# Attention and routed experts on one core: the fifth unit's scores move into a shared PSUM bank, and minima go head by head

## The chip, the cores and the metric

The kernel runs on one core of a Trainium2 chip. The metric is the time of one execution in microseconds, on the device. TensorE (PE) multiplies matrices into PSUM, which has eight banks of 128 partitions by 512 float32 columns here; VectorE (DVE), ScalarE (ACT) and GpSimd (POOL) work on what lies there and in SBUF; SyncE (SP) issues the loads. Each engine runs its own instructions in their order and waits on semaphores for the others.

## The reference, cut to what matters

```
scores = scale * q @ k.T                        # B=8, H=8, S=576, D=64
scores = where(0 <= i - j < 128, scores + slope_h * -|i - j|, -1e9)
attn   = exp(scores - max) / (sum + 1e-9)       # per row
x      = (attn @ v), heads side by side         # 4608 x 512
choice = greedy routing of x @ w_gate, 8 experts with 576 places each
out[e's rows] = relu(x[rows] @ w1[e]) @ w2[e]
```

Only the attention is touched by the change. Since the window is 128 wide, a block of 64 queries meets three blocks of 64 keys at most.

## The kernel before

**Pairs and units.** Two heads h = 0, 1 of one batch are a pair; there are 32 pairs n, four to a batch. Of a pair, q and k lie in one tile with head h on partitions 64h to 64h+63, which is the row group of PE that its matmuls use. The nine blocks of 64 queries are grouped in five units. Units 0 to 3 hold two blocks each, r = 0 and r = 1, and each head's scores of them fill one bank, s[0] or s[1], block r on partitions 64r and up. Unit 4 holds the one block that is left, for both heads: its scores lie in s[0] on partitions 0 to 63 for head 0, and in s[1] on partitions 64 to 127 for head 1, behind the columns of units 0 and 1. It has 192 columns in the pairs of even batches and 64 in those of odd batches; unit 0 has 128 and 192.

**Scores come in two halves** (`UNITS`, L22): units 2 and 3, then units 0, 1 and 4. `scores(n, half)` (L106) takes two banks of `ps_s`, which has only these two, so each half reuses the banks of the half before once its minima have been read; pairs 0 and 1 take banks of `ps_t` for their second half. Its matmuls alternate between the heads (`HR`): (h, r) = 00, 10, 01, 11.

**Minima.** `least(n, units)` (L122) is one DVE instruction for each unit and head, which scales the scores, adds the bias, writes the result to `u` and the row's minimum to `mn` (an accumulator read follows each, as an instruction of its own). Unit 4 takes two such instructions of 64 partitions, since its two heads lie in two banks. `exps` (L138) makes the weights in place, on ACT. Both go unit by unit, head 0 and head 1 in turn.

**One iteration n of the loop** puts on PE, in this order: the transposes of units 2, 1 and 3 of pair n-2 (`turn`, L150, each into a `ps_t` bank, pt); `natural(n-4)` (L224), the output turned back, ten passes named pt L53; the transposes of unit 0 of n-2; the first half of the scores of n; the 64 x 64 transposes of unit 4 of n-2; `av(n-3)` (L167), weights times values, into two banks of `ps_x`, x[0] and x[1]; and the second half of the scores of n. On DVE stand, in the same iteration: minima of units 0 and 1 of n-1, the copy PT1 of unit 1's transposes (`turned`, L162), the minima of unit 4 of n-1, the copy PT3, the minima of units 2 and 3 of n, `divide(n-4)`, and small steps of the router. ACT copies x of n-4 out (L213) and the transposes of units 2 and 0, beside the exponentials; POOL moves 64 columns of that copy (L215).

**What sets the order.** The program keeps the written order on each engine (`put`). Which bank of `ps_t` a tile gets follows the order in which banks come free. A bank x[0] uses its columns 0 to 319 alone. Every float32 matmul shows as two passes in the trace.

The first lines of `scores` and the one of `unit` that place unit 4:

```
        s = [bank() if half and n < 2 else ps_s.tile([128, 512], F32, name="s") for _ in range(2)]
        for t in UNITS[half]:
...
        if t == 4:
            return ms, 64 * m0 + 192, 128 * m0 + 384, 1216 - 64 * ms
```

## Time and profile before

| | us |
|---|---|
| three runs | 699.79, 700.03, 702.93 |
| their median | 700.03 |
| the profiled execution | 701.81 |
| its span in the trace | 700.0 |
| PE busy | 667.7 (95%) |
| PE weight loads busy (PEld) | 589.3 (84%) |
| DVE busy | 465.1 (66%) |
| ACT busy | 326.8 (47%) |
| POOL busy | 152.0 (22%) |
| minima, L133, 308 instructions, mean 332 ns | 88.6 |
| exponentials, L144, 288 instructions, mean 436 ns | 123.9 |
| scores, L53, 1112 passes, mean 327 ns | 65.8 |

The attention fills about the first 214 us of the span; the rest is the last of the routing and the two layers of the experts. The shares of the page are taken over the whole span and don't say what limits the attention. That is read from the chain of waits and the timelines of that stretch, where a row gives the start of a group of instructions, the time from its start to its end, the engine, the line and the tiles. PE's passes overlap, so the time of one (327 ns) is far longer than the time from one to the next.

### The profile page before, as it was taken

What the parts mean: (1) busy time and instruction counts of PE and PEld (TensorE: products, weight loads), DVE (VectorE), ACT (ScalarE), POOL (GpSimd) and SP (SyncE); (2) the same over time, 40 slices, a digit from 0 to 9 for tenths busy, and PEclk for the clock granted to TensorE, in tenths of its full rate; (3) what the DMA queues carried; (4) which work ended last, traced back from release to release, by engine and by line L of the source; (5) the groups of instructions that cost most, each with busy time, mean ns of one, the idle gap of its engine ahead of it and who ended that gap; (6) DMA issues with size and microseconds to landing.
All of it is one profiled execution on the core that took longest, in us unless ns stands there. A gap on an engine that the chain in (4) does not pass through costs nothing.

```text
span 700.0 us, 18965 instructions
## 1 busy us (share of the span) xinstructions
PE 667.7 (95%) x7266; PEld 589.3 (84%) x7267; DVE 465.1 (66%) x1940; ACT 326.8 (47%) x991; POOL 152.0 (22%) x337
## 2 busy tenths in 40 slices
PE   8999999999992899999999999999999999999996
PEld 4899999998981688789788889889988988988985
DVE  5789888888977889699578829828846524523210
ACT  6798888888952344234133233214314324323210
POOL 4022221222220303223250231132133023011011
PEclk8999999999996899999999999999999999999998
DMA  8456575665421725435064234146135325301001
GB/s 297 147 177 208 177 222 175 218 197 180 160 71 45 231 73 189 165 123 209 34 210 133 79 111 160 60 135 181 35 128 162 114 91 154 104 30 38 1 24 49
DMA packets 35139, 92.72 MB, mean 132 GB/s; under 512 B 3808, under 2 KB 13152, under 8 KB 35040
## 3 DMA queue, kind: packets, MB, share of 16 engines
q1 hardware_dynamic: 29152, 72.55, 31.9%
q0 software_dynamic: 5888, 18.88, 8.3%
q8 instruction: 59, 0.97, 0.6%
q14 instruction: 40, 0.33, 0.1%
HBM read 72.54 MB, written 18.87 MB: 131 GB/s over the span
## 4 chain that ended last, share of the span: by engine, by line
PE 84%; DVE 9%; issue 3%; DMA 2%; ACT 1%; SPq 0%; POOL 0%; POOLq 0%; DVEq 0%
PE ph L951 25%; PE po L980 10%; PE po L981 10%; PE s L53 8%; PE po L983 8%; PE pt L157 6%; PE pt L53 6%; PE x L53 6%; PE pg L928 2%; DVE hl L895 2%; DMA raw<-in_w_dram 1%; DVE u L133 1%; DVE hlo L962 1%; ACT hl L893 1%; PE x L1134 1%
## 5 line engine op out<-in xcount | busy, mean ns | idle before, releaser
L951 PE MATMUL ph<-xh,hl 128*128 128x288 f32 (+2 forms) x1024 | 189.7, 298 | 0.0
L951 PEld LDWEIGHTS ph<-xh,hl 128*128 128x128 f32 x1024 | 154.3, 189 | 1.0
L980 PE MATMUL po<-hl,hh 128*128 128x512 f32 (+1 forms) x328 | 130.7, 398 | 0.0
L144 ACT ACTIVATE u<-u,mn 128x192 f32<-128x192 f32 (+2 forms) x288 | 123.9, 436 | 6.2 <-DVE mn L133 6.0
L981 PE MATMUL po<-hl,hh 128*128 128x512 f32 (+1 forms) x328 | 126.4, 385 | 0.0
L951 PE MATMUL ph<-xl,hl 128*128 128x288 f32 (+2 forms) x512 | 115.7, 298 | 0.0
L957 ACT ACTIVATE hh<-ph 128x288 fp32r<-128x288 f32 (+2 forms) x128 | 46.9, 408 | 145.7 <-PE ph L951 139.6
L133 DVE CUSTOM_DVE_ANT_0 u<-s,bm 128x192 f32<-128x192 f32 x308 | 88.6, 332 | 27.0 <-PE s L53 14.8
L983 PE MATMUL po<-hl,hlo 128*128 128x512 f32 (+1 forms) x264 | 102.0, 386 | 0.0
L895 DVE TENSOR_TENSOR hl<-raw,hl 128x512 fp32r<-128x512 f32 x128 | 84.8, 682 | 13.2 <-ACT hl L893 12.8
L992 POOL DMA_INDIRECT out_dram<-o,idx x40 | 43.8, 1094 | 203.2 <-ACT o L987 125.0
L951 PEld LDWEIGHTS ph<-xl,hl 128*128 128x128 f32 x512 | 84.1, 189 | 0.1
L932 DVE TENSOR_TENSOR xl<-pg,xh 128x512 fp32r<-128x512 f32 (+1 forms) x37 | 23.7, 640 | 83.7 <-ACT xh L931 82.6
L962 DVE SCALAR_TENSOR_TENSOR hlo<-ph,hh 128x288 fp32r<-128x288 f32 (+2 forms) x128 | 49.8, 416 | 40.7 <-ACT hh L957 39.5
L893 ACT CAST hl<-raw 128x1024 fp32r<-128x1024 f32 x64 | 65.5, 1049 | 16.6 <-DMA raw<-in_w_dram 10.8
L980 PEld LDWEIGHTS po<-hl,hh 128*128 128x128 f32 x328 | 61.7, 188 | 11.1
L981 PEld LDWEIGHTS po<-hl,hh 128*128 128x128 f32 x328 | 61.8, 188 | 10.6
L53 PE MATMUL s<-qk 64*64 64x192 f32 (+1 forms) x1112 | 65.8, 327 | 1.1 <-DVE mn L133 0.6
L987 ACT COPY o<-po 128x512 f32<-128x512 f32 (+1 forms) x33 | 18.9, 573 | 95.0 <-PE po L983 60.1
L904 POOL DMA_INDIRECT g<-x,idx x40 | 43.8, 1095 | 83.4 <-PE pg L928 33.8
L983 PEld LDWEIGHTS po<-hl,hlo 128*128 128x128 f32 x264 | 49.6, 188 | 10.1
L157 PE MATMUL pt<-ident_sb,u 128*128 128x128 f32 x368 | 53.7, 282 | 1.9 <-DVE PT L165 1.5
(233 smaller groups left out, 925.2 us busy)
## 6 DMA issues: line engine op xcount, KB each, us to landing
raw<-in_w_dram SPq DMA_DIRECT2D x64, 512.0 KB, 3.4
qk<-in_qk_dram SPq DMA_DIRECT2D x32, 576.0 KB, 5.0
v<-in_v_dram SPq DMA_DIRECT2D x32, 288.0 KB, 4.0
x<-xb SPq DMA_DIRECT2D x14, 512.0 KB, 3.6
x<-xb SPq DMA_DIRECT2D x8, 128.0 KB, 2.8
x<-xb SPq DMA_DIRECT2D x4, 256.0 KB
g<-x,idx POOLq DMA_INDIRECT x40
out_dram<-o,idx POOLq DMA_INDIRECT x40
```

What stands on the lines that cost most here:

```text
L53: put(nc.tensor.matmul(out, w, a, start=start, stop=stop, skip_group_check=True))
L133: put(nc.vector.tensor_tensor_reduce(out=u[rows], in0=x[rows, c:c + 64 * m].rearrange("q (j k) -> q j k", k=64), in1=bm[n % NP][rows, y:y ...
L144: put(nc.scalar.activation(u, u, AF.Exp, bias=st["mn"][:, i:i + 1], scale=-1.0, accum_out=st["sm"][:, i:i + 1]))
L157: put(nc.tensor.transpose(ps[:, c:c + 128], u[:, o + 128 * j:o + 128 * j + 128], ident))
L893: self.last = nc.scalar.copy(hl[:, 0, :], raw)
L895: nc.vector.tensor_tensor(hl[:, 1, c:c + 512], raw[:, c:c + 512], hl[:, 0, c:c + 512].bitcast(F32), ALU.subtract)
L951: nc.tensor.matmul(pp[t], w[:, a, j, fo:fo + 128], x[:, j, cut[t]:cut[t + 1]], start=(j == 0 and a == 0 and x is xh), stop=(j == 3 and a = ...
L957: nc.scalar.activation(o, pp[t], AF.Relu)
L962: nc.vector.scalar_tensor_tensor(d, pp[t][:, c0:c1], 0.0, o[:, c0:c1].bitcast(F32), ALU.max, ALU.subtract)
L980: nc.tensor.matmul(out, a, wh, start=(f == 0), stop=False)
L981: nc.tensor.matmul(out, a, wl, start=False, stop=(f == 7 and t == 4))
L983: nc.tensor.matmul(out, hl[:, f, 128 * t:128 * t + 128], wh, start=False, stop=(f == 7))
```

## The change

Four things are changed, all in `scores`, `least` and `exps` and what they call.

- Unit 4's scores, of both heads, go to free columns (320 and up) of an output bank: x[0] of pair n-3, into which `av` has written just before on the same engine. Pairs 0 to 2 take a bank of `ps_x` of their own for it.
- The second half is computed in the order unit 4, unit 0, unit 1.
- The matmuls of a unit go (h, r) = 01, 00, 10, 11, and minima and exponentials go head by head: both units of head 0 and then both of head 1 (`parts`).
- Unit 4's minimum is one DVE instruction over 128 partitions, with one accumulator read, where two of 64 partitions stood.

```
@@ -19,7 +19,7 @@
 NB = S // 64
 NT = N // 128
 LAG = 2
-UNITS = (2, 3), (0, 1, 4)
+UNITS = (2, 3), (4, 0, 1)
 QKW, BMW, XW = 1152, 1216, 144
 
 
@@ -45,7 +45,7 @@
     ident, wn = C["ident"], C["wn"]
     state, bm, batch, late = {}, {}, {}, []
     hs = [slice(64 * h, 64 * h + 64) for h in range(2)]
-    HR = [(h, r) for r in range(2) for h in range(2)]
+    HR = [(0, 1), (0, 0), (1, 0), (1, 1)]
 
     put = tc.keep_in_program_order
 
@@ -84,7 +84,7 @@
         if t == 1:
             return 3, 64 * m0, 128 * m0, 0
         if t == 4:
-            return ms, 64 * m0 + 192, 128 * m0 + 384, 1216 - 64 * ms
+            return ms, 320, 128 * m0 + 384, 1216 - 64 * ms
         return 3, 192 * (t - 2), 128 * m0 + 64 * ms + 384 * (t - 1), 0
 
     def weights(n, t, h):
@@ -111,37 +111,40 @@
             st["mn"] = sb.tile([128, 9], F32, name="mn", bufs=4)
             st["sm"] = sb.tile([128, 9], F32, name="sm", bufs=6)
         s = [bank() if half and n < 2 else ps_s.tile([128, 512], F32, name="s") for _ in range(2)]
+        if half:
+            st["fifth"] = state[n - LAG - 1]["x"][0] if n > LAG else ps_x.tile([128, 512], F32, name="x")
         for t in UNITS[half]:
             m, c = unit(n, t)[0:2]
             w = 64 * m
             for h, r in HR if t < 4 else ((0, 0), (1, 1)):
                 qb, kb, _ = keys(n, t, r)
-                mm(s[h][hs[r], c:c + w], q[hs[h], 64 * qb:64 * qb + 64], k[hs[h], 64 * kb:64 * kb + w])
+                out = s[h] if t < 4 else st["fifth"]
+                mm(out[hs[r], c:c + w], q[hs[h], 64 * qb:64 * qb + 64], k[hs[h], 64 * kb:64 * kb + w])
         st["s"] = s
 
+    def parts(units):
+
+        return [(t, h) for h in range(2) for t in units if t < 4 or h == 0]
+
     def least(n, units):
 
         st = state[n]
-        s = st["s"]
-        for t in units:
-            for h in range(2) if t < 4 else (0,):
-                m, c, _, y = unit(n, t)
-                y += 512 * h
-                i = 2 * t + h
-                u = weights(n, t, h)
-                for rows, x in ((slice(0, 128), s[h]),) if t < 4 else ((hs[0], s[0]), (hs[1], s[1])):
-                    put(nc.vector.tensor_tensor_reduce(out=u[rows], in0=x[rows, c:c + 64 * m].rearrange("q (j k) -> q j k", k=64),
-                                                       in1=bm[n % NP][rows, y:y + 64 * m].rearrange("q (j k) -> q j k", k=64),
-                                                       scale=-0.125, scalar=3e38, op0=ALU.add, op1=ALU.min,
-                                                       accum_out=st["mn"][rows, i:i + 1]))
+        for t, h in parts(units):
+            m, c, _, y = unit(n, t)
+            y += 512 * h
+            i = 2 * t + h
+            x = st["s"][h] if t < 4 else st["fifth"]
+            put(nc.vector.tensor_tensor_reduce(out=weights(n, t, h), in0=x[:, c:c + 64 * m].rearrange("q (j k) -> q j k", k=64),
+                                               in1=bm[n % NP][:, y:y + 64 * m].rearrange("q (j k) -> q j k", k=64),
+                                               scale=-0.125, scalar=3e38, op0=ALU.add, op1=ALU.min,
+                                               accum_out=st["mn"][:, i:i + 1]))
 
     def exps(n, units):
         st = state[n]
-        for t in units:
-            for h in range(2) if t < 4 else (0,):
-                i = 2 * t + h
-                u = weights(n, t, h)
-                put(nc.scalar.activation(u, u, AF.Exp, bias=st["mn"][:, i:i + 1], scale=-1.0, accum_out=st["sm"][:, i:i + 1]))
+        for t, h in parts(units):
+            i = 2 * t + h
+            u = weights(n, t, h)
+            put(nc.scalar.activation(u, u, AF.Exp, bias=st["mn"][:, i:i + 1], scale=-1.0, accum_out=st["sm"][:, i:i + 1]))
 
     def place(n, t, j):
 
```

**PE, the second half of the scores of pair 16** (s are its two banks, x_2173 and x_2159 output banks, qk the tile of q and k, pt_2236 and pt_2223 the next transposes). Before, behind the last product of `av`:

```order
L53 MATMUL x_2173<-PT3_1982,v_1810 64x64 x2
L53 MATMUL s_2206<-qk_1941 64x128 [waits DVE_49,PE_49]
L53 MATMUL s_2207<-qk_1941 64x128 [waits DVE_49,PE_49]
L53 MATMUL s_2206<-qk_1941 64x128
L53 MATMUL s_2207<-qk_1941 64x128
L53 MATMUL s_2206<-qk_1941 64x192
L53 MATMUL s_2207<-qk_1941 64x192
...
L157 MATMUL pt_2236<-ident_sb_61,u_1995 128x128 x3
```

And now:

```order
L53 MATMUL x_2160<-PT3_1970,v_1800 64x64 x2
L53 MATMUL x_2159<-qk_1930 64x192 x2
L53 MATMUL s_2193<-qk_1930 64x128 [waits DVE_49,PE_49]
L53 MATMUL s_2193<-qk_1930 64x128
L53 MATMUL s_2194<-qk_1930 64x128 [waits DVE_49,PE_49]
L53 MATMUL s_2194<-qk_1930 64x128
L53 MATMUL s_2193<-qk_1930 64x192 x2
L53 MATMUL s_2194<-qk_1930 64x192 x2
L160 MATMUL pt_2223<-ident_sb_61,u_1983 128x128 x3
```

Unit 4's two matmuls stand at the front and wait for nothing. The wait for the minima of head 1 is on the fifth matmul of the half, where it was on the second; the wait of head 0 is for the second minimum of its half, where it was for the third.

**PE, the transposes of pair 0 at the start** (pt_227 and pt_228 are unit 2, the next two units 1 and 3, pt_252 unit 0; s_258 is the first bank of pair 2's scores). Before:

```order
L157 MATMUL pt_227<-ident_sb_61,u_125 128x128 [waits DVE_49,DMAHW2_49,PE_49,Activation_49]
L157 MATMUL pt_231<-ident_sb_61,u_125 128x128 [waits DVE_49,PE_49,Activation_49]
L157 MATMUL pt_235<-ident_sb_61,u_125 128x128 [waits DVE_49]
L157 MATMUL pt_252<-ident_sb_61,u_125 128x128 [waits DVE_49]
L53 MATMUL s_258<-qk_158 64x192 [waits DMAHW4_49]
```

And now:

```order
L160 MATMUL pt_228<-ident_sb_61,u_125 128x128 [waits DVE_49,DMAHW2_49,PE_49,Activation_49]
L160 MATMUL pt_232<-ident_sb_61,u_125 128x128 [waits PE_49,Activation_49]
L160 MATMUL pt_236<-ident_sb_61,u_125 128x128 [waits DVE_49,PE_49]
L160 MATMUL pt_252<-ident_sb_61,u_125 128x128 [waits DVE_49,PE_49]
L53 MATMUL s_258<-qk_159 64x192 [waits DMAHW4_49]
```

The waits on DVE of units 3 and 0 keep their places and change what they are for, since other banks of `ps_t` come free first: unit 3's was for the end of the copy PT1 and is for unit 1's minimum of head 0 of pair 1; unit 0's was for a minimum of unit 4 of pair 1, behind PT1, and is for unit 1's minimum of head 1, ahead of PT1.

**DVE, at the same place: the last minima of pair 1 with the copies PT1 and PT3** (pt_200 and pt_201 hold its second half, x_202 is unit 4's bank now). Before:

```order
L133 ISA u_179,mn_180<-pt_201,bm1_162 128x3x64
L133 ISA mn_180 128x1
L165 COPY PT1_245<-pt_231 128x384 [waits PE_49]
L133 ISA u_179,mn_180<-pt_200,bm1_162 64x192 [waits Pool_49]
L133 ISA mn_180 64x1
L133 ISA u_179,mn_180<-pt_201,bm1_162 64x192
L133 ISA mn_180 64x1
L165 COPY PT3_250<-pt_235 128x384 [waits PE_49]
```

And now:

```order
L137 ISA u_179,mn_180<-pt_201,bm1_163 128x3x64
L137 ISA mn_180 128x1
L168 COPY PT1_246<-pt_232 128x384 [waits PE_49]
L137 ISA u_179,mn_180<-x_202,bm1_163 128x192 [waits Pool_49]
L137 ISA mn_180 128x1
L168 COPY PT3_250<-pt_236 128x384 [waits PE_49]
```

Between the two copies stands one minimum with its accumulator read, where two stood. `av` of the next pair takes the bank in which unit 4's scores lay for its x[1], so its first product there, its third matmul, carries a wait on DVE for that minimum.

## Rows read from the trace of the kernel before

**Rows 1.** chain of waits, 84 to 150 us: shares by engine and line

```profile
by line: PE s L53 29.5%; PE pt L157 24.0%; PE pt L53 23.8%; PE x L53 22.8%; issue 0.1%
```

**Rows 2.** same chain: start us, us, engine, tile, line, count; one POOL timeline

```profile
102.96 1.15 PE s L53 x20
...
109.16 1.19 PE s L53 x20
...
121.43 0.90 PE s L53 x18
...
127.72 0.79 PE s L53 x18
...
139.61 1.03 PE s L53 x17
...
145.59 1.04 PE s L53 x17
...
147.77 1.37 PE pt L53 x10
...
148.34 0.23 POOL L215 COPY xT<-xT 128x64 f32<-128x64 f32 x1
```

**Rows 3.** timeline of PE: start us, us, engine, line, op, out<-in, form, count

```profile
131.25 0.91 PE L53 MATMUL s<-qk 64*64 64x192 f32 x16
...
131.95 0.49 PE L53 MATMUL pt<-ident_sb,u 64*64 64x64 f32 x10
```

**Rows 4.** timeline: copies of unit 1, transposes of unit 0, [idle <-releaser]

```profile
105.62 0.55 DVE L165 COPY PT<-pt 128x384 f32<-128x384 f32 x1
...
106.30 0.49 PE L157 MATMUL pt<-ident_sb,u 128*128 128x128 f32 x3
...
130.28 0.55 DVE L165 COPY PT<-pt 128x384 f32<-128x384 f32 x1
...
130.88 0.20 PEld L157 LDWEIGHTS pt<-ident_sb,u 128*128 128x128 f32 x2 [0.23 <-DVE PT L165]
```

**Rows 5.** timeline of DVE: unit 4's first minimum, the next copy

```profile
123.77 0.34 DVE L133 CUSTOM_DVE_ANT_0 u<-s,bm 64x192 f32<-64x192 f32 x1
...
124.55 0.56 DVE L165 COPY PT<-pt 128x384 f32<-128x384 f32 x1
```

**Rows 6.** waits: us, times, longest; PEld in 40:190, DVE in 20:215

```profile
PEld s L53 <- DVE mn L133: 1.6, 9, 0.2
...
DVE u L133 <- PE s L53: 11.4, 15, 1.1
```

**Rows 7.** timeline of the start; last row from the chain of waits

```profile
11.17 0.55 PE L157 MATMUL pt<-ident_sb,u 128*128 128x128 f32 x3 [0.40 <-ACT u L144]
...
12.17 0.55 DVE L165 COPY PT<-pt 128x384 f32<-128x384 f32 x1
...
12.78 0.80 PE L157 MATMUL pt<-ident_sb,u 128*128 128x128 f32 x5 [1.07 <-DVE PT L165]
...
13.51 1.56 PE L53 MATMUL s<-qk 64*64 64x192 f32 x16
...
16.30 2.29 PE L53 MATMUL s<-qk 64*64 64x128 f32 x20 [0.59 <-DVE mn L133]
...
18.52 1.33 PE L157 MATMUL pt<-ident_sb,u 128*128 128x128 f32 x5
...
25.28 1.14 PE pt L157 x9
```

**Rows 8.** timeline of ACT at the start

```profile
19.46 0.48 ACT L165 COPY PT<-pt 128x384 f32<-128x384 f32 x1 [1.42 <-PE pt L157]
...
22.73 0.53 ACT L165 COPY PT<-pt 128x448 f32<-128x448 f32 x1 [0.70 <-PE pt L53]
...
25.02 0.67 ACT L213 COPY xT<-x 128x320 f32<-128x320 f32 x2
```

**Rows 9.** windows: us, busy PE PEld DVE ACT POOL, clock, DMA, GB/s

```profile
13.40:20.20 6.80, 6.21 (x58) 4.93 (x57) 3.05 (x18) 5.38 (x23) 0.97 (x6) 0.50 0.73 260
```

## The prediction

> **What bounds the kernel now.** I read three views in this order: the chain of waits of the attention's steady part, the waits of PE and DVE there, and the timeline of the start.
>
> The chain from 84 to 150 us is PE in all its shares, four lines of it, and 0.1% issue [rows 1]: there the time is PE's, and only what PE computes or waits for counts. A pair takes 6.2 us (109.16 less 102.96) [rows 2]. DVE waits for scores 11.4 us in 15 long gaps [rows 6], so it is not the bound, but its minima free the two banks that the next scores go into. The reader should see the second halves of the scores in the chain: 0.90 us in pair 19 and 0.79 in pair 20 (the narrower unit 4), but 1.15 and 1.19 in pairs 16 and 17 and 1.03 and 1.04 in 22 and 23 [rows 2]. The extra 0.24 to 0.29 is PE's second matmul, which stands behind the minimum of head 1 and holds all that follows. In the whole trace 12 pairs show it, 6 to 9, 14 to 17 and 22 to 25: two pairs at either side of a change of batch width.
>
> The start is different. Up to about 27 us ACT, DVE and PE wait for one another: PE waits 1.07 us for the copy PT1 at 12.78 and 0.59 for a minimum at 16.30 [rows 7], ACT is idle 1.42 us ahead of 19.46 and 0.70 ahead of 22.73 [rows 8], and from 13.40 to 20.20 the clock granted to PE is 0.50, the lower of its two levels [rows 9].
>
> **Steady pairs: the second head's wait.** Now two matmuls of unit 4 and two of head 0 stand ahead of the wait for head 1, and head 0 waits for the second minimum of its half instead of the third. The 16 passes of a first half start over 0.70 us, from 131.25 to 131.95 [rows 3], so a matmul of 192 columns (two passes) is worth about 0.09 us of PE when four run at once, and up to 0.35 alone (two times 0.175, four times 0.70 over 16). What each stalled pair gets back is limited by what is late next:
> - Pairs like 17: about 0.24 of its 0.29, since unit 4's and head 0's passes fill the wait and nothing else is late.
> - Pairs like 16: the transposes of unit 0 at 106.30 wait for PT1, which starts at 105.62. Where PE really waited for PT1, it went on 0.60 behind that copy's start (130.28 to 130.88); here it starts 0.68 behind it [rows 4]. So PE may come forward by only 0.08.
> - Pairs like 22: unit 4 has 64 columns, a third of the cover, so 0.12 of 0.24.
> - Pairs like 23: 0. The natural product behind it takes 1.37 (147.77) and ends on POOL's copy of 148.34 to 148.57 [rows 2], which hangs on the divide and not on these scores.
>
> Three rounds of (0.24 + 0.08 + 0.12 + 0) are 1.3 us. The first halves wait on minima too, for unit 4's, which the change takes out of those banks. PE's weight loads of scores show 1.6 us of waiting on minima in 9 places [rows 6], most of it in second halves; I take 0.3 for the rest (between 0 and 1.6). Steady term: **1.6 us**, between 0 and 3.
>
> **Steady pairs: what costs nothing.** The passes are as many as before. The 32 minima and 32 accumulator reads that go lie on DVE: in an even batch unit 4 falls from 0.78 (123.77 to 124.55) to one of its two instructions, 0.39 [rows 5], which shortens an engine that waits for PE's scores anyway. The exponentials of unit 3's head 0 and unit 2's head 1 trade places, and PE needs them an iteration later.
>
> `av` gets a new wait on DVE, for unit 4's minimum, with the rest of `av`, the second half and the next transposes queued behind it. `av` is 22.8% of 66 us [rows 1] over 10.6 pairs, so 1.4 us; it stands ahead of the second half at 127.72 [rows 2], so it starts near 126.3. Unit 4's minima of that iteration were done by 124.55 [rows 5]: 1.8 us of cover. If DVE came that late, the price would be what is missing, pair by pair.
>
> **The order of the passes on PE.** The order 01, 00, 10, 11 puts the matmuls of one row group next to each other. No row shows it; the nearest is the 0.70 us for 16 passes in the old order [rows 3]. With four at a time a pass is 0.175 there; were the packing a tenth better or worse, both halves (0.70 and 0.85) would move by 0.15 us a pair, 5 us in all. The nearest row of neighbours in one bank and on both row groups, the 64 x 64 transposes (131.95) [rows 3], shows ten passes in one run beside scores, without a gap. I take 0, and keep plus and minus 2 us, less than half of that tenth.
>
> The Trainium skill, "TensorE: Matmul & The Clock Gate", Part 3, states that a weight load overlaps with matmuls in flight only if its row group differs; taken word for word, the new order would expose loads that the old one hides. By that rule the sum below turns into the slower case that is worked out from rows below.
>
> **The start.** DVE's chain there is continuous up to PT1 at 12.17 [rows 7]. Unit 4 of pair 0 saves 0.39 on it [rows 5], and the minima of pair 1 end at 11.78. Unit 1's transposes (11.17, waiting for ACT) don't move. The transposes of units 3 and 0, which started behind PT1 at 12.78, now wait for minima of pair 1 that are done by then, and follow at once: eight passes at 0.12 (nine took 1.14 at 25.28) from 11.17 on. So the first half of pair 2 starts near **12.1** instead of 13.51, at full clock, where a half starts over 0.70 us [rows 3] instead of lasting 1.56 [rows 7].
>
> On DVE PT1 then ends at 12.33, unit 4's minimum at 12.72, PT3 at 13.27, and the four minima of pair 2 at 14.5 (four took the 1.2 from 15.07, where the first half ended, to 16.30 [rows 7], so 0.3 each). There the second half's last wait is over, 1.8 us earlier. It takes 2.22 at the low clock (16.30 to 18.52) [rows 7]; eight of its twenty passes now stand ahead of the wait, which leaves 1.4, so the next transposes come near 15.9 instead of 18.52, 2.6 earlier.
>
> From there to the next transposes at 25.28 it was 6.76 us [rows 7]. About 1.0 of waits goes (ACT's idle 0.70, and some 0.3 around its copy at 25.02 [rows 8]), but 2.6 us more of this round lie in the slow stretch, if that still ends at 20.2, and half of that, 1.3, is lost. So 22.96 instead of 25.28: **2.3 us**. ACT sets a ceiling: its idle 1.42 and 0.70 [rows 8] plus 0.7 between the end of its copy, 25.69, and the end of the transposes, 26.42 [rows 7], behind which PE first needs that copy: 2.8. The term lies between 1.0 (only the wait of 1.07 for PT1 goes [rows 7]) and 2.8.
>
> **The sum.** The profiled execution took 701.81 us (span 700.0), 1.78 above the median of 700.03. 701.81 - 1.6 - 2.3 = 697.9 for a profiled run; the same 3.9 off the median gives **696.1 us**, 0.56% faster. What a measurement of this kernel can tell from no change is about 0.5%, 3.5 us: the forecast stands close to that bound, at 696.5. Its own range is 694.5 to 697.7.
>
> **The rivals.**
> - *Only the start gains*: 697.7. For it: half of the stalled pairs already have another wait close behind, as said of 16 and 23. Against: pair 17 has none.
> - *Only the steady pairs gain*, since ACT or the low clock takes the start's gain back: 698.4. For it: ACT's chain is nearly continuous and 6.21 of the 6.80 us at low clock are PE busy [rows 9]. Against: ACT's 2.1 us of idle.
> - *The low clock falls on more work*: were a second stretch of this kind granted, or this one longer by its own length, the 6.21 us of PE work in it [rows 9] would cost up to half of that, 3.1: 699.2. For it: PE's activity ahead of 13.40 is what changes. Against: PE becomes busier there, not less.
> - *Nothing to measure*: 700.0. The waits move to other releasers.
> - *The passes pack better in the new order*: a tenth of 1.55 us a pair at most, three in the middle: 693.
> - *Slower: unit 4's two matmuls run one after the other.* They go to one bank from two row groups. In a half that runs four at once they would stand alone: 0.35 us for 192 columns and 0.12 for 64, 16 pairs each, plus 7.5 us: **703.5**. It decides from 0.23 us a pair on (7.5 over 32), where the gain is gone by as much as is told apart. Against: the 64 x 64 transposes write one bank from both row groups, and `av` does 68 passes in 1.4 us in two banks.
>  The Trainium skill, "TensorEngine Tiling (Array Packing)", Gotcha 1, states that different row tiles cannot access the same PSUM bank at once; the rows of the transposes and of `av` speak against it here.
> - *Slower: the same row group behind itself.* If only two of four quadrants run at a time, both halves double, 1.55 us a pair, 50 us: 746. Against: each matmul's two passes are neighbours of one row group already, and 16 of them start in 0.70 us [rows 3].
>
> **How the numbers follow.** Chances: forecast 0.48; only the start 0.13; only steady 0.10; low clock 0.08; nothing 0.07; packing 0.07; one bank 0.04; row group 0.03. Faster by over 0.5% (below 696.5): about 0.7 of the forecast's, the packing's and a fifth of the start's, 0.44. Slower by over 0.5%: 0.07, and 0.01 of the clock's; the rest, 0.48, is within. The range from 693.5 to 699.6 leaves out the slower cases, half of "nothing" and the far half of the packing, about 0.16.
>
> **What would show it.** In the profile after: the first half of pair 2 near 12.1 and the transposes two iterations on near 23.0; second halves of 0.90 to 0.95 us in pairs like 17; no wait of first halves on minima; 288 minima. Wrong would be: `av` waiting for DVE, halves that take over 0.75 or 0.95 us without a wait (packing), the low clock beyond 20.2, or ACT without idle time and the 25.28 unmoved.

## The result, and the profile of the changed kernel

| | before | changed |
|---|---|---|
| median, us | 699.91 (4 runs, 698.65 to 702.93) | 692.06 (4 runs, 691.12 to 692.76) |
| profiled execution, its span | 701.81, 700.0 | 692.76, 691.0 |
| DVE busy, instructions | 465.1, 1940 | 453.4, 1876 |
| ACT busy | 326.8 | 325.1 |
| PE busy | 667.7 | 660.8 |

The changed kernel is faster by 7.85 us: the ratio is 0.988 (95% interval 0.985 to 0.991). Later comparisons of the same two kernels gave 0.989 (0.986 to 0.993) and 0.988 (0.984 to 0.992). The forecast was 3.9 us (696.1), its range began at 693.5: the sign was right, the size half of what came.

The steady part first. The chain of waits from 80 to 146 us shows, as before [rows 1], PE in all its shares:

```profile
by line: PE x L53 26.0%; PE s L53 25.7%; PE pt L53 24.3%; PE pt L160 24.0%
```

The scores, s, fell from 29.5% of that stretch to 25.7%, but unit 4's passes are counted with x now, which rose from 22.8% to 26.0%. The two together went from 52.3% to 51.7%. Pair 22, whose second half took 1.03 us in the chain of before (139.61) [rows 2], looks like this on PE's timeline, first before and then changed (start us, us, engine, line, operation, out<-in, form, count):

```profile
139.43 1.21 PE L53 MATMUL s<-qk 64*64 64x192 f32 x20
140.57 0.33 PE L157 MATMUL pt<-ident_sb,u 128*128 128x128 f32 x1
```

```profile
134.91 0.34 PE L53 MATMUL s<-qk 64*64 64x192 f32 x1
...
134.97 0.29 PE L53 MATMUL x<-qk 64*64 64x64 f32 x4
135.05 0.87 PE L53 MATMUL s<-qk 64*64 64x192 f32 x15
135.85 0.33 PE L160 MATMUL pt<-ident_sb,u 128*128 128x128 f32 x1
```

Unit 4's four passes, into x, are mixed with the last of `av` and with head 0's, and from the first score (134.91 us) to the transposes it is 0.94 us with no idle time of the weight loads in it; in before it was 1.14 (139.43 to 140.57). The waits of weight loads from 36 to 184 us, the answer to [rows 6], have no line for scores behind minima any more:

```profile
PEld pt L160 <- issue: 6.7, 24, 0.3
PEld s L53 <- issue: 4.2, 25, 0.2
PEld pt L53 <- POOL xT L218: 0.8, 4, 0.2
PEld pt L160 <- ACT u L147: 0.3, 1, 0.3
```

What has gone there is the name and not the time. The same view of before, from 36 to 190 us, has two more lines for scores beside the one of [rows 6]:

```profile
PEld s L53 <- issue: 1.7, 10, 0.2
PEld s L53 <- DVE PT L165: 1.0, 6, 0.2
```

With the 1.6 us in 9 places that are put down to minima, that is 4.3 us in 25 places before and 4.2 us in 25 places now. It is a gap of about 0.17 us ahead of the first halves, and both kernels have it.

And DVE, from 20 to 209 us, waits for scores 30.6 us where the two lines of before, behind s [rows 6] and behind the transposes that follow the scores, made 22.6; one wait is new. The second line of before, and then the changed kernel:

```profile
DVE u L133 <- PE pt L53: 11.2, 14, 1.1
```

```profile
DVE u L137 <- PE s L53: 30.6, 28, 3.3
...
DVE u L137 <- ACT xT L216: 1.4, 1, 1.4
```

The start, PE's timeline, answers [rows 7]:

```profile
10.86 1.13 PE L160 MATMUL pt<-ident_sb,u 128*128 128x128 f32 x8 [0.41 <-ACT u L147]
11.92 0.88 PE L53 MATMUL s<-qk 64*64 64x192 f32 x16
...
13.73 1.32 PE L53 MATMUL s<-qk 64*64 64x128 f32 x16 [0.26 <-DVE mn L137]
14.98 1.42 PE L160 MATMUL pt<-ident_sb,u 128*128 128x128 f32 x11
16.33 0.88 PE L53 MATMUL s<-qk 64*64 64x192 f32 x16
...
19.72 1.20 PE L160 MATMUL pt<-ident_sb,u 128*128 128x128 f32 x9
22.63 2.56 PE L53 MATMUL pt<-wn_sb,xT 128*128 128x144 f32 x10 [1.71 <-ACT xT L216]
...
25.54 1.24 PE L53 MATMUL s<-qk 64*64 64x192 f32 x16
```

The transposes of units 1, 3 and 0 run in one piece (10.86), pair 2's scores begin at 11.92 (forecast 12.1, before 13.51), and the transposes that were forecast for 22.96 come at 19.72. Then PE waits 1.71 us for ACT's copy of the output, which stands at 22.16 behind the exponentials of pair 3. And the clock, in windows (us, busy PE PEld DVE ACT POOL, granted clock, DMA share, GB/s):

```profile
13.40:20.20 6.80, 6.42 (x149) 5.37 (x148) 5.65 (x35) 6.80 (x31) 1.04 (x6) 1.00 0.86 314
...
23.00:24.00 1.00, 1.00 (x6) 1.00 (x5) 0.55 (x3) 1.00 (x6) 0.00 (x0) 0.50 0.53 212
24.00:25.00 1.00, 1.00 (x6) 0.99 (x6) 0.00 (x0) 1.00 (x6) 0.00 (x0) 0.50 0.07 28
```

The stretch at 0.50, the lower of the two levels, which lay at 13.40 to 20.20 in before [rows 9], is gone from there; a shorter one stands behind the 1.71 us wait. Such a stretch is called a slow stretch from here on.

**Where the 7.85 us are.** The stretch from one pair's first scores to the next pair's is called a round here. Four marks on PE's timeline cut the span: the first scores of pair 0, those of pair 4, those of pair 31, and the first product of `av` of pair 31.

| stretch | before | changed | difference |
|---|---|---|---|
| start: scores of pair 0 to pair 4 | 21.77 | 19.57 | -2.2 |
| steady: pair 4 to pair 31 | 164.48 | 160.86 | -3.6 |
| end: pair 31 to its `av` | 13.95 | 13.05 | -0.9 |

Up to that `av` (206.22 and 199.45) it is 6.8 us. The rest, to the end of the span, differs by 2.2 us in these two executions (493.8 and 491.6), of which 1.3 are the time behind the last product (7.00 and 5.66 us); over three profiles of each kernel that time is between 5.7 and 7.0 for both, so this part is taken for scatter.

### The profile page after: what moved, and what is told of

Its sections match the earlier page's. It is cut to its first block, busy times and chain, and to the rows that moved or that the text cites. A ratio compares the mean times of both kernels' runs of the same rounds, so it can differ in the third digit from the quotient of the medians.

```text
span 691.0 us, 18850 instructions
## 1 busy us (share of the span) xinstructions
PE 660.8 (96%) x7266; PEld 581.2 (84%) x7267; DVE 453.4 (66%) x1876; ACT 325.1 (47%) x991; POOL 152.4 (22%) x337
## 3 DMA queue, kind: packets, MB, share of 16 engines
HBM read 72.54 MB, written 18.87 MB: 132 GB/s over the span
## 4 chain that ended last, share of the span: by engine, by line
PE 85%; DVE 7%; DMA 4%; ACT 2%; issue 1%; SPq 0%; POOL 0%; POOLq 0%; DVEq 0%
PE ph L954 26%; PE po L983 10%; PE po L984 10%; PE po L986 8%; PE s L53 7%; PE x L53 7%; PE pt L53 7%; PE pt L160 6%; PE pg L931 2%; DMA raw<-in_w_dram 2%; DVE hl L898 1%; ACT hl L896 1%; ACT u L147 1%; PE m L589 1%; DMA rel_sb<-in_rel_dram 1%
## 5 line engine op out<-in xcount | busy, mean ns | idle before, releaser
L137 DVE CUSTOM_DVE_ANT_0 u<-s,bm 128x192 f32<-128x192 f32 (+1 forms) x248 | 71.8, 346 | 32.4 <-PE s L53 31.7
L896 ACT CAST hl<-raw 128x1024 fp32r<-128x1024 f32 x64 | 65.5, 1049 | 17.1 <-DMA raw<-in_w_dram 12.1
L53 PE MATMUL s<-qk 64*64 64x192 f32 (+1 forms) x992 | 60.5, 327 | 0.6 <-DMA qk<-in_qk_dram 0.3
L147 ACT ACTIVATION_READ_ACCUMULATOR u<-u,mn 128x1 f32 x288 | 55.8, 194 | 0.0
```

The lines of the kernel that those rows point to most:

```text
L53: put(nc.tensor.matmul(out, w, a, start=start, stop=stop, skip_group_check=True))
L137: put(nc.vector.tensor_tensor_reduce(out=weights(n, t, h), in0=x[:, c:c + 64 * m].rearrange("q (j k) -> q j k", k=64), in1=bm[n % NP][:, y ...
L147: put(nc.scalar.activation(u, u, AF.Exp, bias=st["mn"][:, i:i + 1], scale=-1.0, accum_out=st["sm"][:, i:i + 1]))
L896: self.last = nc.scalar.copy(hl[:, 0, :], raw)
```

## The experiments

All were profiled. What is compared is the same marks, which agree within 0.1 us in the steady stretch between executions of one kernel without a slow stretch in it (before 164.47 to 164.49, changed 160.39 and 160.44; the 160.86 of the first profile has the end of the slow stretch in pair 4's round and 0.1 more at pair 19). The times scatter more (before 695.5 to 708.6 us over the sessions), and back the marks up but for the first run below.

**The change for the first three pairs only, and from pair 3 on only.** A condition on the pair chooses the bank, the order of the half, the head order and the form of the minimum.

```
-            st["fifth"] = state[n - LAG - 1]["x"][0] if n > LAG else ps_x.tile(...)
+        if half and new(n):                  # new(n): n < 3
+            st["fifth"] = ...
```

> All of the change for pairs 0 to 2 only; from pair 3 on as in the kernel before. Theory 'two terms': the start's gain (pair 4's first half began 2.25 us earlier in the changed kernel, 25.54 for 27.79) comes from these three pairs and is carried to the end, the 3.6 us of the later pairs are absent: the first half of pair 4 near 25.5, of pair 31 near 190.0, time near 697.6 where before is 699.9. Rival 'one chain': the start's gain is only kept because the later pairs keep up, and is lost by pair 10: pair 31 near 192, time near 699.5.

Measured: pair 4 at 25.22, pair 31 at 190.14, steady 164.92, so nothing of the steady gain; time 699.4 against 700.8 of before, ratio 0.9995 (0.997 to 1.002). The steady part is as in before but for 0.4 us more at pair 7, once. The gain of 1.4 us in the median is within the interval of no change. So the marks came where 'two terms' put them, and the time where the rival did: this run does not show by its time that the start's gain is kept to the end.

> All of the change from pair 3 on only; pairs 0 to 2 as in the kernel before. Theory 'two terms': pair 4's first half stays near 27.8, and pair 31's comes 3.6 us earlier than before, near 188.7; the last stage of the attention gives its 0.9 too; time near 695.4. Rival 'one chain': the later pairs gain only what the start leaves them, less than 2 us: pair 31 at 190.5 or later, time above 697.

Measured: steady 160.41, the whole steady gain; the end 13.05; time 695.7, ratio 0.993 (0.989 to 0.996). 'Two terms' holds for the steady part. But pair 4 came at 24.56 where 27.8 was expected, though its first three pairs are those of before: this execution had no stretch at the low clock. That opened the question of the start.

**The heads alternate again, all else changed.**

```
-    HR = [(0, 1), (0, 0), (1, 0), (1, 1)]
+    HR = [(h, r) for r in range(2) for h in range(2)]
-        return [(t, h) for h in range(2) for t in units if t < 4 or h == 0]
+        return [(t, h) for t in units for h in range(2) if t < 4 or h == 0]
```

> The changed kernel with the matmuls, minima and exponentials of units 0 to 3 in the old order, the heads alternating; unit 4 stays in the output's bank, first in its half, with one minimum. Theory 'cover': what hides the wait for head 1's minimum is what stands ahead of it on PE, and without head 0's two matmuls that is unit 4's alone, so the second halves of pairs like 22 (64 columns) keep about 0.12 of their stall of 0.25, those like 17 about none; pair 31 near 187.6 to 188.2, time near 693.5. Rival 'bank': the gain comes from unit 4's minima leaving the two banks, so the head order is worth nothing: pair 31 within 0.4 of 186.4, time near 692.

Measured: steady 160.80, against 160.4 with the new order. The rival holds almost: the head order is worth 0.4 us on top of the rest. Unit 4's two matmuls at the front are enough even in pairs like 22 (a round of 5.77 us, changed 5.75, before 5.99), where they have 64 columns. By the forecast's figures they were too short for that, so something else had to have shortened the wait. Time 693.6, ratio 0.991 (0.988 to 0.994).

**Only the head order, on the kernel before.**

> The kernel before with the matmuls, minima and exponentials of units 0 to 3 head by head; unit 4 stays in the two score banks, last, with two minima. Theory 'cover': head 0's two matmuls ahead of head 1's wait hide about half to all of the 0.25 in the 12 stalled pairs, 1.5 to 3 us; the first halves go on waiting for unit 4's minima; start unchanged (27.8 for pair 4); pair 31 near 190, time near 697.5. Rival 'bank': nothing or less than 0.5 us, pair 31 at 192, time near 699.5.

Measured: steady 163.45 (a second profile 163.51), a gain of 1.0; time 697.6, ratio 0.996 (0.993 to 0.999). Less than 'cover' asked, more than 'bank'. Pairs like 22 kept their round (5.97 for 5.99), and those like 17 gained 0.17. Neither theory explains that: the 0.17 is gained in the first half, where the first minimum starts 1.02 us behind the scores, as in the other pairs, and 1.19 before. Head 0's two matmuls ahead of the wait for head 1 gave nothing that can be told.

**Unit 4 last in its half.** `UNITS = (2, 3), (0, 1, 4)`.

> The changed kernel with unit 4's two matmuls at the end of the second half again. Theory 'cover': head 0's two matmuls alone hide the wait for head 1 as far as 64 columns of unit 4 would, and the last piece of the half is longer; from pair 4 to pair 31 near 161.8 (0.9 more than the changed kernel), if unit 4's part of the cover matters at the even pairs 8, 9, 16, 17, 24, 25 with 0.1 to 0.15 each. Rival: head 0's two matmuls and the earlier minima are enough, 160.9 to 161.2.

Measured: steady 161.31, 0.9 more than the changed kernel, the sum that 'cover' said, though not by the pairs that it named: 0.15 in pair 17 and 0.11 in 22, but 0.03 in 16. Time 693.9, ratio 0.992 (0.989 to 0.996).

**Unit 4's minimum in two instructions of 64 partitions.**

```
-            put(nc.vector.tensor_tensor_reduce(out=weights(n, t, h), in0=x[:, c:c + 64 * m]...
+            for rows in (slice(0, 128),) if t < 4 else hs:
+                put(nc.vector.tensor_tensor_reduce(out=u[rows], in0=x[rows, c:c + 64 * m]...
```

> The changed kernel with unit 4's minimum as two instructions of 64 partitions. Theory: DVE is not the bound in the steady part, so from pair 4 to pair 31 it is 160.9 to 161.2; at the start DVE's chain is 0.3 to 0.4 longer per pair, which moves pair 2's first half from 11.9 to 12.2 at most. Rival: unit 4's minimum stands ahead of the copy PT3 and of the next minima, and pairs of the stalled kind get back 0.2 each of their wait: 162.5 or more.

Measured: steady 160.41: the 32 instructions that went are worth nothing there. The end was 13.49 instead of 13.05, and the start 18.32, as in the changed kernel without a slow stretch, though pair 2 came at 12.39, later than the 12.2 that was allowed for. Time 692.6, ratio 0.990 (0.986 to 0.993).

**The bank alone**: the old head order and unit 4 last, so that only its place in the output's bank and its one minimum are left.

> The changed kernel with the old head order everywhere and unit 4 last in its half: what is left is unit 4's scores in the output's bank, and their one minimum. The first minimum of each first half waits for PE alone here, where before it waits for PE and ACT. Theory 'second wait': in the stalled pairs that minimum starts 0.91 to 0.93 us after the first scores instead of 1.04, so the bank alone gives 0.1 in each of 12 stalled pairs and takes the waits of the first halves away: 162.3 to 162.8 us from pair 4 to pair 31 (before 164.5, changed 160.4). Rival 'order': the bank alone gives nothing to the second halves, and the first minimum starts at 1.04 as before: 163.5 or more.

Measured: steady **161.67**, 2.8 of the 4.1 us, more than the 162.3 to 162.8 of 'second wait' gave, since the pairs without a stall gained 1.1 too; time 695.6, ratio 0.995 (0.991 to 0.998). DVE's timeline shows why. Of pair 22, the first minimum of its first half, before, in this kernel, and with the head order alone ([idle <-releaser] at the end):

```profile
138.31 0.36 DVE L133 CUSTOM_DVE_ANT_0 u<-s,bm 128x192 f32<-128x192 f32 x1 [0.62 <-PE pt L53]
```

```profile
132.94 0.36 DVE L137 CUSTOM_DVE_ANT_0 u<-s,bm 128x192 f32<-128x192 f32 x1 [0.97 <-PE s L53]
```

```profile
134.71 0.36 DVE L133 CUSTOM_DVE_ANT_0 u<-s,bm 128x192 f32<-128x192 f32 x1 [0.61 <-PE pt L53]
```

The scores that it reads began at 137.26, 132.01 and 133.69: it starts 1.04, 0.93 and 1.02 us behind them (from the trace's nanoseconds; the rows are rounded). Before, this instruction waits for two engines, PE and ACT, and an instruction of its own that only waits stands ahead of it:

```profile
L133 DVEq EVENT_SEMAPHORE  x1: 21/21/21, 138.2 to 138.2; - x1
```

It starts 0.94 us behind the scores, which is when the minimum itself starts without it, and the minimum follows 0.10 us later. The ACT step that is waited for, an exponential of a pair four iterations back (`u` and `mn` have four buffers), was long done, and does not set the time: it is 1.04 in 23 of the 28 pairs from 4 on, and 0.93 in all 28 with the bank alone. With unit 4 in the output's bank that unit's minimum carries the wait for ACT (for the copy out of the bank), which is ahead of PE's scores anyway, and the first minimum waits for PE alone. It starts 0.11 us earlier, all four follow, and the second half shrinks by as much in the chain of waits: from 1.03 to 0.92 us in pair 22, from 1.04 to 0.93 in pair 23. No run changed this wait alone, but two others share the effect out: with the new head order it is 1.024 us with the second wait and 0.915 without (the changed kernel), and unit 4's minimum in two instructions leaves the 0.915 as it is.

The second half of pair 22 shows what each part of the change does. PE goes on when the first weight load of head 1 is released, which stands here:

```profile
139.62 0.13 PEld L53 LDWEIGHTS s<-qk 64*64 64x64 f32 x1
```

```profile
135.02 0.13 PEld L53 LDWEIGHTS s<-qk 64*64 64x64 f32 x1
```

All times in us, the first two behind the first score of the pair:

| kernel | first minimum | head 1's load | from that load to the transposes |
|---|---|---|---|
| before | 1.042 | 2.357 | 0.950 |
| head order alone | 1.024 | 2.340 | 0.943 |
| bank alone | 0.932 | 2.247 | 0.950 |
| changed, heads alternating | 0.931 | 2.247 | 0.835 |
| changed, unit 4 last | 0.915 | 2.231 | 0.944 |
| changed | 0.915 | 2.230 | 0.829 |

The bank takes 0.11 off the release, the head order 0.02. Behind the release only unit 4's place counts: at the front of the half, its matmul of head 1 no longer stands there, and that is 0.11 to 0.12. Head 0's matmuls ahead of the wait leave that time as it is.

**How often the slow stretch comes.** Six more profiles of kernels with either start, four of them of the two kernels unchanged.

> The kernel before, unchanged, for a second profile. Theory 'draw': the stretch at clock 0.50 from 13.4 to 20.2 us is not a property of the kernel but differs between executions, since a kernel whose first three pairs are as before (from_three) had none; then a second profile may have none or another one, and without it pair 4's first half begins near 24.6 to 25.0 instead of 27.79 and pair 31's near 189.3. Rival 'fixed': the stretch is there again at 13.4, pair 4 at 27.8, pair 31 at 192.3.

Measured: 21.70 us from pair 0 to pair 4, clock 0.53 from 13.4 to 20.2. 'Fixed', so far; time 699.5.

> The changed kernel, unchanged, for a second profile and more times on this chip. Theory 'draw': without a slow stretch at the start pair 4's first half begins near 24.2 (as in old_heads), pair 31's near 185.0; with one, up to 2 us later. From pair 4 to pair 31 it is 160.9 us in either case, 3.6 less than before's 164.5. Rival 'fixed': 25.5 and 186.4 again. Time of either: 0.988 to 0.992 of before.

Measured: no slow stretch before 200 us, 18.62 us from pair 0 to 4, steady 160.39. 'Draw'; time 692.2.

> The kernel before, unchanged, for a third profile of its start. Theory 'every time': the gap of 1.07 us that PE waits at 11.7 us, with what stands behind it, brings the stretch at clock 0.50 in each execution of this program; pair 4's first half at 27.7 to 27.8. Rival 'draw': it is there in some executions only; without it pair 4's first half is 19.0 to 19.2 us behind pair 0's (21.7 with it), near 25.0.

Measured: the stretch again, but shorter (from 12.8 to 16): 20.36 us.

> The kernel with the change from pair 3 on, for a second profile: its first three pairs are those of the kernel before. Theory 'every time': these three pairs' gap and work decide the clock, and the first profile, without a slow stretch, was the exception: pair 4's first half 21.5 us behind pair 0's. Rival 'draw': without it, 19.0 us, or with it, from one execution to the next.

Measured: the stretch is there this time, 21.31 us: 'draw', for the same program had none in its first profile. Time 693.2.

> The kernel before with minima and matmuls head by head, a second profile: its start is that of the kernel before, pair 2's first half 7.49 us behind pair 0's. Theory 'mostly': the slow stretch comes at 13 us (as in 4 of 6 profiles of kernels with this start), pair 4's first half 20.4 to 21.8 us behind pair 0's. Rival: it is not there, 19.1.

Measured: not there, as in its first profile; 19.28 us.

> The changed kernel, unchanged, a third profile and times beside the kernel above. Theory 'rare': no stretch at clock 0.50 before 27 us, pair 4's first half 18.3 to 18.7 us behind pair 0's. Rival 'as often as before': such a stretch as in the first profile, 19.5 or more.

Measured: none, 18.43 us; time 691.6.

The windows from 13.4 to 20.2 us of two kernels with one start, before_again and heads_only:

```profile
13.40:20.20 6.80, 6.21 (x59) 4.93 (x59) 2.94 (x18) 5.20 (x23) 0.94 (x5) 0.53 0.71 246
```

```profile
13.40:20.20 6.80, 5.64 (x102) 4.50 (x102) 5.13 (x30) 6.79 (x31) 1.17 (x7) 1.00 0.77 285
```

In both, pair 2's scores begin 7.49 us behind pair 0's, so the order of work up to there is the same; the count behind PE's time tells what the clock did to it, 59 passes or 102 in 6.8 us. Pair 0 to pair 4 over all of these:

| start | with a slow stretch, us | without, us |
|---|---|---|
| old (before three times, from_three and heads_only twice each) | 21.77, 21.70, 20.36, 21.31 | 18.97, 19.14, 19.28 |
| new (changed three times, old_heads, two_minima) | 19.57 | 18.62, 18.43, 18.34, 18.32 |

Without it the new start is 0.7 us shorter (19.1 less 18.4). The slow stretch cost the old start 1.2 to 2.6 us in four of seven profiles, and the new one 1.1 us in one of five. What brings it in one execution and not in another with the same work isn't settled by these runs. In the old start PE stood idle 1.07 us ahead of it [rows 7], in the new one 1.71; but the changed kernel's second profile had the same idle time, 1.72, and no slow stretch behind it, and all seven profiles of the old start have the 1.06 or 1.07, also the three without the stretch. No run changed such a gap alone. The kernels with a start between the two are left out of the table (first_three 19.19, fifth_last 19.09, bank_only 19.21, none with a slow stretch).

**ACT as the ceiling of the start.** First the copy of pair 0's output was moved ahead of pair 3's exponentials of units 2 and 3 (and taken from its old place in the next iteration).

```
+            if not LAG < n <= SOONER:        # SOONER = 3
                 exps(n, UNITS[0])
...
+        if LAG < n <= SOONER:
+            copy_out(k - 1)
+            exps(n, UNITS[0])
         ...
             scores(n, 1)
```

> The changed kernel with one thing moved: ACT copies pair 0's output out ahead of the exponentials of units 2 and 3 of pair 3, where it stood behind them. Theory 'ACT is the bound of the start': PE's natural product of pair 0, which waited for this copy, comes 1.7 us earlier, pair 4's first half 17.0 us behind pair 0's instead of 18.6 and the end 1 to 1.7 us earlier: time 690.5 to 691.2 where the changed kernel has 692.1. Rival: the delayed exponentials are late for the next iterations and give it back by pair 6: within 0.5 us of the changed kernel.

Measured: 18.55 us from pair 0 to 4, nothing gained. PE's timeline shows the wait at another place:

```profile
20.81 0.38 PE L54 MATMUL x<-qk 64*64 64x192 f32 x2 [1.97 <-ACT xT L217]
```

Unit 4's scores go to the bank that is being copied, and now stood behind the copy in the program's order. Times: 693.7, ratio 0.993 (0.990 to 0.995), no better than the changed kernel. Then the same two lines were put behind `scores(n, 1)`.

> The changed kernel with ACT's copy of pair 0's output ahead of the exponentials of units 2 and 3 of pair 3, and written behind the second half of pair 3's scores, so that unit 4's scores, which go to the bank that is copied, don't wait for the copy (in 'sooner' they did, 1.97 us). Theory 'ACT is the bound of the start': the natural product of pair 0 starts near 20.8 instead of 22.5, pair 4's first half 16.9 us behind pair 0's (18.6 in the changed kernel), kept to the end: time near 690.7 (changed kernel 692.1). Rival: the delayed exponentials give it back: 18.3 or more by pair 4, or a longer round at pairs 5 and 6, and 692.

Measured: the natural product starts at 21.18 instead of 22.54, but the next step finds ACT late again:

```profile
21.18 1.41 PE L54 MATMUL pt<-wn_sb,xT 128*128 128x144 f32 x10
23.33 0.44 PE L161 MATMUL pt<-ident_sb,u 128*128 128x128 f32 x2 [0.74 <-ACT PT L169]
23.70 0.88 PE L54 MATMUL s<-qk 64*64 64x192 f32 x16
```

Pair 3 to pair 4 took 7.07 us instead of 7.97 (changed, second profile), 0.9 less of the 1.7 hoped for. But pair 2 came 6.91 us behind pair 0 in this execution and 6.24 in that one, so pair 4 came at 18.41 behind pair 0, where the rival put it. Time 691.9 against 691.6 for the changed kernel in the same session: no difference can be told. Moving one of ACT's copies moved the wait from one consumer to the next; from 12.0 to 22.6 us ACT has no idle time in the changed kernel (10.60 of 10.60 us busy).

## Why the prediction was right in sign and wrong in size

**The steady term was mis-sized: 1.6 us forecast, 4.1 measured** (164.48 to 160.4, without the slow stretch). Of its two parts the one for the stalled pairs lacks a piece in every pair:

| pairs like | forecast | measured, round of before to changed |
|---|---|---|
| 22 | 0.12 | 0.24 (5.99 to 5.75) |
| 23 | 0 | 0.13 (6.14 to 6.01) |
| 16 | 0.08 | 0.17 (6.10 to 5.93) |
| 17 | 0.24 | 0.43 (6.14 to 5.71) |

Three times 0.97 is 2.9 where three times 0.44 were counted. The step that failed is the one on DVE: that it "is not the bound", and that what the change takes from it "shortens an engine that waits for PE's scores anyway". So the end of the minima was taken as given. But they start 0.11 us earlier because a second wait left the first of them, and 0.02 more by the head order, and PE's wait for their end is shorter by that 0.13 in each of the 12 pairs, 1.6 us. The order of instructions shows it: that minimum waits for PE and ACT before and for PE alone now. The prediction looked at the waits of PE's instructions and not at those of DVE's.

Without the 0.13, and without 0.15 of the first half in pairs like 17, what is left is 0.11, 0, 0.04 and 0.15, 0.9 us over three rounds: what unit 4's place at the front is worth by itself (161.67 to 160.80, and 161.31 to 160.4). The limits of the forecast, 1.3 us, were near that and a little too wide. Their reason holds for unit 4 alone; head 0's matmuls, which were to fill the wait too, gave nothing.

The part for the first halves, 0.3 us, rested on a misread line. The nine waits of [rows 6] stand ahead of first halves, not of second ones, and their time stays. What the first halves lost is another wait, for unit 4's minimum of head 1: in pairs 9, 17 and 25 the second matmul stood 0.17 us behind the first, and the first minimum came 0.15 later for it, 0.45 us in all.

The other pairs gained up to 0.16 each, 1.2 us in all, where nothing was counted. The divide comes as much earlier as the minima, and with it POOL's copy, for which the natural product waits in rounds 11, 19 and 27 (6.29 for the last, now 6.17). In rounds 12, 20 and 28 (6.12 for the last, now 6.00) the transposes of unit 0 wait for PT1, which comes earlier too: 0.23 us of idle time before, 0.12 now. Pair 23 was put at 0 for the wait of the natural product on POOL. It did take part of the gain: the product became 1.49 us (pair 15, in the chain of waits) where it was 1.37 [rows 2]:

```profile
95.21 1.49 PE pt L53 x10
```

But the copy moved as well, so 0.13 were left. Together the pieces are 1.6, 0.9, 0.45 and 1.2 us, the 4.1. By parts of the change, the bank gave 2.8, unit 4's place at the front 0.9 and the head order 0.4.

**The start: 2.3 forecast, 2.2 measured, for another reason.** Pair 2 came at 11.92 (forecast 12.1) as worked out. What failed is the step in which the slow stretch keeps its place up to 20.2. It isn't a part of the start that work is moved through, but comes or doesn't. That 2.2 lies so near to 2.3 is luck. Over three profiles each, before took 21.28 us on average and the changed kernel 18.87; 0.7 of these 2.4 is the order of work, and 1.7 is the clock. Whether the change makes the stretch rarer (three profiles of three before, one of three changed) these few executions don't show. The ceiling of 2.8, made from ACT's idle time, was made from idle time that the slow stretch itself had caused: without it ACT has none (heads_only, with the old start, 6.79 of 6.80 us busy), and in the changed kernel PE waits for ACT's copy (the 1.71 above). The rival "the low clock falls on more work" is not borne out: there was less of the low clock in the changed kernel's profiles, not more.

**The end: 0.9 us that no step had.** Before, a step of the divide on DVE waits for PE until 203.75; the router's step stands behind it, and behind that step's matmuls on PE the product of pair 31. In the changed kernel the divide goes on at once:

```profile
201.70 1.39 PE L53 MATMUL pt<-wn_sb,xT 128*128 128x144 f32 x10
...
203.46 0.23 PE L53 MATMUL pt<-ident_sb,u 64*64 64x64 f32 x2
```

```profile
203.07 0.20 DVE L240 RECIPROCAL rs<-sd 128x10 f32<-128x10 f32 x1
203.75 0.25 DVE L248 TENSOR_TENSOR Lp<-pt,rs 128x48 f32<-128x48 f32 x1 [0.47 <-PE pt L53]
```

```profile
196.58 0.21 DVE L243 RECIPROCAL rs<-sd 128x10 f32<-128x10 f32 x1
196.89 0.25 DVE L251 TENSOR_TENSOR Lp<-pt,rs 128x48 f32<-128x48 f32 x1
```

The kernels with unit 4 in the output's bank in their last pairs have an end of 12.9 to 13.1 (two_minima 13.49), first_three 13.42, before and the head order alone 13.95. In before the wait ends with the 64 x 64 transposes (203.46 and 0.23), though the natural product ahead of them had ended at 203.09; in the changed kernel the step starts at 196.89, ahead of these transposes (197.36). Why the step waits for the later ones in before was not taken apart.

**What was right.** The edits that were costed at nothing were nothing: `av`'s new wait for unit 4's minimum never holds it in the changed trace; the one instruction less on DVE gives nothing in the steady part (two_minima 160.41); the new head order does nothing to the packing of PE's passes, for the first halves take 0.71 us from first score to what follows, before 0.70. So the rule of the Trainium skill, "TensorE: Matmul & The Clock Gate", Part 3, on weight loads of one row group does not show here. The rule of the Trainium skill, "TensorEngine Tiling (Array Packing)", Gotcha 1, on row tiles and one PSUM bank, does not either: unit 4's four passes take 0.29 us in one bank from both row groups (134.97), and the first passes of the two heads start 0.01 us apart. Both slower rivals fell with that.

One figure was too high with no consequence: unit 4's minimum was put at 0.39, half of two, and is 0.27 (11.92 to 12.19 on DVE). The Trainium skill, "VectorE: DVE Perf Modes", section "Two Vector instructions with no wait between them", says that an instruction whose operands start in another group of 32 partitions than the last one's is held until that one has finished. The trace agrees: the two halves, on partitions 0 to 63 and 64 to 127, took 0.39 each [rows 5], more than one of all 128, and the second started at 124.15, when the first had ended (123.77 and 0.34).

## What to carry to other kernels

Read the waits of every engine's instructions in the changed order, not only of the one that sets the end: a tile that moves to another bank takes its waits along, and an instruction that had to wait for two engines may wait for one. What a stall on the path is worth is the sum of what covers it and of how much earlier its releaser comes, and the second part holds for every pair alike. Work put ahead of a wait helps by what it takes from behind the wait: unit 4's matmul did, head 0's did not. Profile a kernel more than once before a stretch at the low clock is taken into a sum: it may not be the kernel's.

## What the runs showed of the hardware

A second semaphore to wait for, even one whose work has long been done, put DVE's minimum 0.11 us later behind PE's scores (1.042 us with it and 0.932 without in the old head order, 1.024 and 0.915 in the new one); with PE stalled on those minima in 12 pairs, that alone is 1.3 us.

The granted clock at the start differed between executions of one program: 1.00 in one profile of from_three from 12.5 to 20.2 us, 0.53 in another from 13.4 to 20.2, with the same instructions. It moved the rest of the attention by 2.3 us (18.97 and 21.31 us from pair 0 to pair 4).
